# Cosformer attention and a multiplicative FFN on one core: the attention steps of batches 2 and 4 to 7 respaced within the FFN's steps

## The chip, the cores and the metric

The kernel runs on one core of one Trainium2 chip. The metric is the device time of one execution in microseconds; the time of a kernel is the median of several executions. Before the change it is 248.72 us, the median of 4 runs from 247.82 to 250.03 us.

## The reference

Inputs are q, k, v of shape (8 batches, 8 heads, 576 positions, 64) in float32 and four weight matrices. Attention is linear (no softmax), with cosine and sine weights by position; its output, 4608 tokens of 512, goes through three matrix products.

```python
def phi(x, c, s):
    r = np.maximum(x, 0.0)
    return np.concatenate([r * c, r * s], axis=-1)       # 64 -> 128 features
q_p = phi(q, cos_w, sin_w)
k_p = phi(k, cos_w, sin_w)
kv = np.einsum('bhsf,bhsd->bhfd', k_p, v)
z = np.sum(k_p, axis=2)
num = np.einsum('bhsf,bhfd->bhsd', q_p, kv)
den = np.einsum('bhsf,bhf->bhs', q_p, z)[..., None] + 1e-06
x = (num / den)                                          # tokens x 512
h = (x @ w1) * (x @ w2) @ w3
out = h @ w_out
```

## The kernel before

The 4608 tokens are 9 FFN tiles of 512. `ffn_groups` (L459) yields once for each step of a tile: 40 steps for tile 0 (which also multiplies w3 by w_out once, w34b), 24 for every other. In a tile from the third on, steps 0 to 15 are the two products of the eight 128-wide blocks in turn (w1b at an even step, w2b at an odd one, L465, four matmuls of 512 columns each) and steps 16 to 23 are the outputs of four blocks of 128 tokens in two halves each (L535, again four matmuls a step: the blocks jc 0 to 3, then 4 to 7 of abT). After a w1b step ScalarE copies the product from PSUM to asb (L518); after a w2b step VectorE multiplies the two into abT (L522); after every second output step ScalarE copies the block to osb (L542). FFN products take their PSUM banks from four in rotation.

Step numbers run through all tiles: tile 1 has the steps 40 to 63, tile 2 those from 64, tile 3 from 88, tile 4 from 112, and so on. The attention of a batch is spread over these steps by hand. `at(s, call)` (L562) puts a call into the list of step s; the loop at the end (L664) runs each step of the FFN and then the calls of that step, so the engines' queues get the instructions in this order. There is no other scheduler. Calls of one step stand in the order in which the plans were made: a batch's own in the order of `plan`, an earlier batch's ahead of a later one's.

`plan` (L572) places a batch's work in five chunks of 128 positions (the last has 64); odd batches begin with the short one:

- `kf`: `prep_k`, features of a k chunk. VectorE makes the cosine half (L273), ScalarE the sine half (L277).
- `qf`: `prep_q`, the same for a q chunk, and then `transpose_q`, a DMA transpose into qpT issued from SyncE's queue (L286).
- `vc`: `prep_v`, the copy of a v chunk into va, on GpSimd from batch 2 on (L300).
- `kv`: `kv_chunk`, eight matmuls on TensorE (L308) accumulated over the five chunks; after the last, ScalarE and VectorE copy the result to kvs (L313, L314).
- `nu`: `num`, the numerators of a chunk: eight matmuls on TensorE with qpT as weights and kvs moving (L368), and on VectorE the division by the denominators (L384 to L386) into xblk; then `x_tr`, a DMA transpose of xblk into the FFN's input xT, again from SyncE (L416).

`plan_loads` (L584) places the six loads of a batch, two halves each of k, q and v (for batch 3 the order is q, k, v). A load is issued from GpSimd's queue (L123, L127; batch 7: L133, L137), behind `hold_back` (L565): ScalarE writes one element, `mark` (L568), and GpSimd copies it, `seen` (L570), so that the load leaves no earlier than ScalarE comes to that place in its queue. Chunks 0 to 3 need both halves of a load, the short chunk one (batch 7: chunks 0 to 3 the first load, the short one the second). k and v have one buffer, q two.

For batches 4 to 7 the steps are given relative to two bases: `last`, the first numerator step of the batch before, and `base`, that of the batch itself (74, 99, 123, 148, 173).

Of the kernel before, what the change touches and what calls it, by code (L numbers as in the profile page):

```python
# [68 lines left out]
def kernel(  # L69
# [41 lines left out]
    def load(b, which, part=None):  # L111
        for name in which:
            src = {"k": k, "v": v, "q": q}[name]
            if b == B - 1:
                if part == 0:
                    raw[b, name] = ld.tile([P, H, NCH, D], BF16, name=name + "s",
                                           bufs=2 if name == "q" else 1)
                (load_first4 if part else load_first)(nc.gpsimd, raw[b, name], src, b=b)
                continue
            if part != 1:  # L120
                raw[b, name] = ld.tile([P, H, NCH, D], BF16, name=name + "s",
                                       bufs=2 if name == "q" else 1)
                nc.gpsimd.dma_start(  # L123
                    out=raw[b, name][0:64, :, :, :].rearrange("p h j d -> p h (j d)"),
                    in_=src[b, :, 0:320, :].rearrange("h (p j) d -> p h (j d)", j=5))
            if part != 0:
                nc.gpsimd.dma_start(  # L127
                    out=raw[b, name][64:128, :, 0:4, :].rearrange("p h j d -> p h (j d)"),
                    in_=src[b, :, 320:S, :].rearrange("h (p j) d -> p h (j d)", j=4))
# [116 lines left out]
    def order_of(b):  # L246

        return [0, 1, 2, 3, 4] if b % 2 == 0 else [4, 0, 1, 2, 3]
# [40 lines left out]
    def prep_k(b, c):  # L289
        features(b, feat_of(b)[0], raw[b, "k"], c)  # L290

    def prep_q(b, c):
        features(b, feat_of(b)[1], raw[b, "q"], c)
        if c in dma_q(b):
            transpose_q(b, c)

    def prep_v(b, c):
        R = ROWS[c]
        eng = nc.vector if b < 2 else nc.gpsimd
        eng.tensor_copy(out=feat_of(b)[2][:R, c, :, 0:D], in_=raw[b, "v"][:R, :, c, :])  # L300

    def kv_chunk(b, c, i):
        kp, qp, va = feat[b]
        if i == 0:
            att_of(b)["kv"] = ps_att.tile([P, 2, 512], FP32, name="pnum")
        kvt = att[b]["kv"]
        for h in range(H):
            nc.tensor.matmul(kvt[:, h // 4, ds((h % 4) * 65, 65)], lhsT=kp[:, c, h, :],  # L308
                             rhs=va[:, c, h, 0:D + 1], start=(i == 0 and h % 4 == 0),
                             stop=(i == NCH - 1 and h % 4 == 3))  # L310
        if i == NCH - 1:
            kvs = sm.tile([P, H, D + 1], BF16, name="kvs", bufs=2)
            nc.scalar.copy(out=kvs[:, 0:4, :], in_=kvt[:, 0, 0:260])  # L313
            nc.vector.tensor_copy(out=kvs[:, 4:8, :], in_=kvt[:, 1, 0:260])  # L314
            att[b]["kvs"] = kvs
# [88 lines left out]
    def x_tr(b, c, by_vector=False):  # L404
        R, rows = ROWS[c], out_rows(b, c)
        xblk = att[b]["x"].pop(c)
        xf = xblk[:].rearrange("p g h d -> p (g h d)")
        if b % 2 == 0:
            slot = S * b + 128 * c
        else:  # L410
            slot = S * b + (0 if c == 4 else 64 + 128 * c)
        t, o = divmod(slot, 512)
        if t not in xT:
            xT[t] = xtp.tile([P, 4, 512], BF16, name="xT")
        if b >= 2 or (b, c) in ((0, 4), (1, 3)):
            nc.sync.dma_start_transpose(out=xT[t][:, :, ds(o, R)], in_=xf[rows])  # L416
            return
        pst = ps_tr.tile([P, 8, 128], BF16, name="pst")
        for kc in range(4):
            nc.tensor.transpose(pst[:, kc, :], xf[:, ts(kc, 128)], identb[:])  # L420
        copy = nc.vector.tensor_copy if by_vector else nc.scalar.copy
        copy(out=xT[t][:, :, ds(o, R)], in_=pst[:, 0:4, rows])
# [139 lines left out]
    def at(s, *calls):  # L562
        slots[s] += calls

    def hold_back():  # L565

        mark = sm.tile([P, 1], BF16, name="mark", bufs=8)
        nc.scalar.copy(out=mark[0:1, :], in_=zeros[0:1, 0:1])  # L568
        seen = sm.tile([P, 1], BF16, name="seen", bufs=1)
        nc.gpsimd.tensor_copy(out=seen[0:1, :], in_=mark[0:1, :])  # L570

    def plan(b, kf, vc, kv, qf, nu, loads=None, xt=None):  # L572
        order = order_of(b)
        for i, c in enumerate(order):
            at(kf[i], lambda c=c: prep_k(b, c))
            at(qf[i], lambda c=c: prep_q(b, c))
            at(vc[i], lambda c=c: prep_v(b, c))
        for i, c in enumerate(order):
            at(kv[i], lambda c=c, i=i: kv_chunk(b, c, i))
        for i, c in enumerate(order):  # L580
            at(nu[i], lambda c=c: num(b, c, in_two=b == 1 and c in (0, 2)))
            at(xt[i] if xt else nu[i], lambda c=c: x_tr(b, c, by_vector=(b, c) == (1, 1)))

    def plan_loads(b, when):  # L584

        for piece, s in zip([(n, half) for n in {2: "kv", 3: "qkv"}.get(b, "kqv") for half in range(2)], when):
            def issue(piece=piece):
                hold_back()
                load(b, *piece)
            at(s, issue)  # L590
# [42 lines left out]
    for jp, s in enumerate((12, 16, 18, 20, 22, 24, 26, 28)):  # L633
# [3 lines left out]
         qf=(29, 30, 30, 31, 31), nu=(35, 36, 38, 39, 42), xt=(37, 38, 40, 42, 42))  # L637
    for c, s in zip(order_of(1), (31, 32, 34)):
        at(s, lambda c=c: q_tr(1, c))
    at(43, no_more_by_pe)  # L640
    plan_loads(2, (27, 28, 33, 35))
    plan(2, kf=(37, 39, 40, 41, 43), vc=(41, 42, 43, 44, 45), kv=(47, 47, 47, 48, 48),
         qf=(41, 42, 44, 45, 46), nu=(49, 51, 53, 55, 58))
    plan_loads(3, (36, 37, 47, 50, 54, 57))
    plan(3, kf=(54, 57, 59, 61, 63), vc=(64, 65, 66, 67, 68), kv=(71, 72, 72, 73, 73),
         qf=(60, 62, 64, 67, 70), nu=(74, 77, 79, 84, 87))

    bases = [74, 99, 123, 148, 173]
    for b, last, base in zip(range(4, B), bases, bases[1:]):
        plan_loads(b, [last + s for s in (-8, -5, 1, 4, 7, 10)])  # L650
        plan(b, kf=[last + s for s in (4, 7, 10, 13, 15)],
             vc=[base + s for s in (-9, -8, -7, -6, -5)],
             kv=[base + s for s in (-4, -3, -3, -2, -2)],
             qf=[base + s for s in (-12, -9, -6, -3, 0)],
             nu=[base + s for s in (0, 2, 5, 8, 11)])

    for i in range(2 * (NT - 1)):
        def put(i=i):
# [41 lines left out]
```

## Time and profile before

| what | value |
|---|---|
| runs | 247.82, 247.9, 249.55, 250.03 us; median 248.72 |
| profiled execution | 250.03 us, span 248.0 us from its first to its last instruction |
| TensorE granted clock | 0.999 of full |
| TensorE busy | 238.8 us, 96% of the span, 1842 matmuls |
| VectorE, ScalarE, GpSimd busy | 55%, 52%, 38% |
| DMA | 41.22 MB, mean 166 GB/s; loads (software queue) 73.7%, transposes (hardware queue) 34.1% of 16 engines' span |
| q and x transposes from SyncE | 33 and 32, median 4.4 and 4.9 us from issue to landing |
| loads of 320 KB (k, q, v) | median 6.3, 6.1 and 6.1 us from issue to landing |

Busy time of each engine, in stretches of 12.4 us (columns: the stretch, its length, busy us and number of instructions of TensorE, its weight loads, VectorE, ScalarE and GpSimd, the granted clock, the DMA engines' share and rate):

```profile
62.00:74.40 12.40, 12.35 (x144) 9.59 (x143) 10.10 (x25) 8.88 (x18) 4.27 (x9) 1.00 0.91 136
74.40:86.80 12.40, 11.48 (x73) 5.49 (x73) 8.22 (x23) 7.25 (x15) 3.04 (x7) 1.00 1.38 173
86.80:99.20 12.40, 12.29 (x97) 6.46 (x98) 6.31 (x12) 6.65 (x15) 4.58 (x10) 1.00 0.99 134
111.60:124.00 12.40, 12.29 (x105) 6.58 (x106) 8.06 (x17) 7.15 (x15) 5.34 (x11) 1.00 1.28 154
124.00:136.40 12.40, 11.76 (x75) 5.59 (x74) 7.28 (x20) 7.09 (x15) 3.36 (x8) 1.00 1.43 139
136.40:148.80 12.40, 12.29 (x105) 6.61 (x106) 7.54 (x18) 7.37 (x16) 4.78 (x11) 1.00 1.18 136
```

Between the first 12 us and the last, a stretch has 12.29 to 12.35 us of TensorE work, but for the two from 74.4 and from 124.0. Where an instruction stands in time is read from the timeline: tile 1 begins near 61 us, tile 2 (step 64) near 86, tile 3 (step 88) near 109.5, tile 4 (step 112) at 133.4, and batch 2's five numerators start at 71.5, 73.6, 75.6, 78.5 and 81.4 us.

### The profile page before, as it was taken

How to read it: one execution, taken by the hardware profiler on the slowest of the kernel's cores; microseconds unless marked ns; L12 is line 12 of the kernel's file. 1: busy time of each engine (PE TensorE's matmuls, PEld its weight loads, DVE VectorE, ACT ScalarE, POOL GpSimd, SP SyncE). 2: the span in 40 equal slices, each digit the busy share in tenths (PEclk: the TensorE clock that was granted, in tenths of full speed). 3: DMA queues.
4: the chain of work that ended last, by engine and by line, in shares of the span. 5: the costliest groups of instructions: out<-in, count | busy, mean ns of one | idle time of the engine just before them, and what ended most of it. 6: DMA issues, size and time to landing. Idle time of an engine off the chain costs nothing.

```text
span 248.0 us, 5010 instructions
## 1 busy us (share of the span) xinstructions
PE 238.8 (96%) x1842; PEld 130.8 (53%) x1872; DVE 137.5 (55%) x344; ACT 130.0 (52%) x266; POOL 93.5 (38%) x196
## 2 busy tenths in 40 slices
PE   8799999999998999999998999999999999999994
PEld 3479555566964445455544555455545554444443
DVE  7775663668967545646664476557464635312420
ACT  2575324856943873466556744855575333434332
POOL 7555352124422261217032612263213005978700
PEclk9999999999999999999999999999999999999999
DMA  7999999999989969999999999999994536898923
GB/s 195 178 197 199 207 205 201 196 181 172 140 131 169 177 103 165 113 143 133 175 123 155 123 149 183 169 123 143 163 143 86 98 63 211 254 283 295 272 104 129
DMA packets 86201, 41.22 MB, mean 166 GB/s; under 512 B 53793, under 2 KB 82721, under 8 KB 86177
## 3 DMA queue, kind: packets, MB, share of 16 engines
q0 software_dynamic: 37008, 27.20, 73.7%
q1 hardware_dynamic: 49168, 13.71, 34.1%
q8 instruction: 14, 0.23, 0.4%
q14 instruction: 11, 0.08, 0.1%
HBM read 38.80 MB, written 9.44 MB: 194 GB/s over the span
## 4 chain that ended last, share of the span: by engine, by line
PE 89%; DMA 6%; issue 2%; DVE 1%; POOL 1%; ACT 0%; POOLq 0%
PE ffnps L465 47%; PE ffnps L535 24%; PE ffnps L240 6%; PE pnum L368 4%; PE pnum L308 3%; DMA qs<-in_q_dram 3%; DMA qpT<-qp 3%; PE pst L226 1%; PE pst L339 1%; PE pst L420 1%; PE ffnps L551 1%; POOL vs L133 0%; DVE xblk L386 0%; PE pfirst L368 0%; ACT asb L518 0%
## 5 line engine op out<-in xcount | busy, mean ns | idle before, releaser
L465 PE MATMUL ffnps<-xT,w2b 128*128 128x512 bf16 (+2 forms) x338 | 75.0, 344 | 0.4
L465 PE MATMUL ffnps<-xT,w1b 128*128 128x512 bf16 (+2 forms) x333 | 74.3, 343 | 1.1 <-issue 0.6
L522 DVE TENSOR_TENSOR abT<-asb,ffnps 128x512 bf16<-128x512 bf16 x64 | 43.9, 686 | 54.2 <-PE ffnps L465 53.7
L518 ACT CAST asb<-ffnps 128x512 bf16<-128x512 f32 x64 | 37.4, 584 | 51.5 <-PE ffnps L465 48.0
L535 PE MATMUL ffnps<-w34b,abT 128*128 128x512 bf16 x271 | 63.7, 379 | 0.4
L465 PEld LDWEIGHTS <-w2b 128*128 128x128 bf16 x344 | 31.2, 98 | 27.8
L465 PEld LDWEIGHTS <-w1b 128*128 128x128 bf16 x344 | 30.5, 98 | 26.3 <-issue 1.1
L570 POOL COPY seen<-mark 1x1 bf16<-1x1 bf16 x50 | 8.9, 178 | 85.4 <-ACT mark L568 85.4
L542 ACT COPY osb<-ffnps 128x512 f32<-128x512 f32 x35 | 20.5, 585 | 38.2 <-PE ffnps L535 37.2
L535 PEld LDWEIGHTS <-abT 128*128 128x128 bf16 x280 | 25.9, 98 | 27.6
L277 ACT ACTIVATE qp<-qs,sinv 128x512 bf16<-128x512 bf16 (+2 forms) x40 | 28.1, 716 | 1.8 <-DMA qs<-in_q_dram 1.8
L300 POOL COPY va<-vs 128x512 bf16<-128x512 bf16 (+1 forms) x30 | 17.8, 627 | 23.6 <-DMA vs<-in_v_dram 23.6
L386 DVE TENSOR_TENSOR xblk<-pnum,den 128x512 bf16<-128x512 f32 (+1 forms) x37 | 25.6, 691 | 1.3
L277 ACT ACTIVATE kp<-ks,sinv 128x512 bf16<-128x512 bf16 (+1 forms) x35 | 24.9, 718 | 0.0
L450 POOL DMA_DIRECT2D out_dram<-osb x42 | 22.1, 531 | 3.0 <-issue 2.0
L368 PEld LDWEIGHTS <-qpT 128*128 128x128 bf16 x320 | 15.3, 98 | 9.8 <-DMA qpT<-qp 1.3
L384 DVE TENSOR_SCALAR den<-pnum 128x8 f32<-128x8 f32 (+1 forms) x37 | 6.0, 163 | 22.0 <-PE pnum L368 21.8
L368 PE MATMUL pnum<-kvs,qpT 128*128 128x65 bf16 x296 | 15.8, 194 | 0.9 <-DMA qpT<-qp 0.8
L273 DVE TENSOR_SCALAR qp<-qs,cosv 128x512 bf16<-128x512 bf16 (+1 forms) x40 | 15.6, 398 | 0.7 <-DMA qs<-in_q_dram 0.6
L240 PE MATMUL ffnps<-woutb,w3T 128*128 128x512 bf16 x61 | 15.1, 379 | 0.2
L308 PEld LDWEIGHTS <-kp 128*128 128x128 bf16 x280 | 11.4, 98 | 4.3
L273 DVE TENSOR_SCALAR kp<-ks,cosv 128x512 bf16<-128x512 bf16 (+1 forms) x35 | 13.0, 377 | 0.8 <-DMA ks<-in_k_dram 0.8
(88 smaller groups left out, 182.8 us busy)
## 6 DMA issues: line engine op xcount, KB each, us to landing
out_dram<-osb POOLq DMA_DIRECT2D x16, 256.0 KB, 4.4
out_dram<-osb POOLq DMA_DIRECT2D x24, 128.0 KB, 3.9
qs<-in_q_dram POOLq DMA_DIRECT2D x8, 256.0 KB, 8.2
ks<-in_k_dram POOLq DMA_DIRECT2D x6, 320.0 KB, 6.3
qs<-in_q_dram POOLq DMA_DIRECT2D x6, 320.0 KB, 6.1
vs<-in_v_dram POOLq DMA_DIRECT2D x6, 320.0 KB, 6.1
ks<-in_k_dram POOLq DMA_DIRECT2D x6, 256.0 KB, 6.8
vs<-in_v_dram POOLq DMA_DIRECT2D x6, 256.0 KB, 5.5
```

Of the source, the lines that this page charges most:

```text
L240: nc.tensor.matmul(acc[:, :], lhsT=w3T[:, lc % 4, :], rhs=woutb[:, lc, :], start=(lc == 0), stop=(lc == 7))
L273: nc.vector.tensor_scalar(out=dst[:R, c, :, 0:D], in0=src[:R, :, c, :], scalar1=0.0, scalar2=cosv[:R, at:at + 1], op0=ALU.max, op1=ALU.mult)
L277: nc.scalar.activation(out=dst[:R, c, 0:n, D:F], in_=src[:R, 0:n, c, :], func=ACTF.Relu, scale=sinv[:R, at:at + 1], bias=0.0)
L308: nc.tensor.matmul(kvt[:, h // 4, ds((h % 4) * 65, 65)], lhsT=kp[:, c, h, :], rhs=va[:, c, h, 0:D + 1], start=(i == 0 and h % 4 == 0), sto ...
L368: nc.tensor.matmul(banks[h // 4][:, ds((h % 4) * 65, 65)], lhsT=qpT[:, h, ds(at, 128)], rhs=kvs[:, h, :], start=True, stop=True)
L386: nc.vector.tensor_tensor(out=xblk[rows, g], in0=n4[:, :, :, 0:D], in1=den[rows, g].unsqueeze(3).to_broadcast([R, G, 4, D]), op=ALU.mult)
L450: eng.dma_start(out=rows[:, :, cols], in_=osb[64 * i:64 * i + rows.shape[0], :, cols])
L465: nc.tensor.matmul(out, lhsT=w[:, kc, ts(jc, 128)], rhs=x[:, kc, tok], start=(kc == 0), stop=(kc == 3))
L518: nc.scalar.copy(out=asb[:], in_=aT[:, :])
L522: nc.vector.tensor_mul(out=abT[:, jc, :], in0=asb[:], in1=bT[:, :])
L535: nc.tensor.matmul(ops[:, :], lhsT=abT[:, jc, ts(ms, 128)], rhs=w34b[:, jc, :], start=(jc == 0), stop=(jc == 7))
L542: nc.scalar.copy(out=osb[:, ms % 2, :], in_=ops[:, :])
```

## The change

Only step numbers change. No instruction is added or removed.

- Batch 2: k features of its last chunk go from step 43 to 44, q features (and transpose) of the third chunk from 44 to 43; kv goes from 47, 47, 47, 48, 48 to 46, 46, 46, 47, 47; the numerators from 49, 51, 53, 55, 58 to 48, 50, 52, 57, 60.
- Batch 3: its k loads go from 47 and 50 to 48 and 51; kv from 71, 72, 72, 73, 73 to 71, 71, 72, 72, 72. Numerators and features stay.
- Batches 4 to 7, relative to their bases: k loads a step earlier, q loads two steps and one step later, v loads the same and a step earlier; k features a step or two earlier and, at the end, two steps apart; v copies one step later and two of them in one step; kv in two steps instead of three; q features every two steps from -10 to -2 instead of every three from -12 to 0; the second numerator a step after the first instead of two.

```diff
-    plan(2, kf=(37, 39, 40, 41, 43), vc=(41, 42, 43, 44, 45), kv=(47, 47, 47, 48, 48),
-         qf=(41, 42, 44, 45, 46), nu=(49, 51, 53, 55, 58))
-    plan_loads(3, (36, 37, 47, 50, 54, 57))
-    plan(3, kf=(54, 57, 59, 61, 63), vc=(64, 65, 66, 67, 68), kv=(71, 72, 72, 73, 73),
+    plan(2, kf=(37, 39, 40, 41, 44), vc=(41, 42, 43, 44, 45), kv=(46, 46, 46, 47, 47),
+         qf=(41, 42, 43, 45, 46), nu=(48, 50, 52, 57, 60))
+    plan_loads(3, (36, 37, 48, 51, 54, 57))
+    plan(3, kf=(54, 57, 59, 61, 63), vc=(64, 65, 66, 67, 68), kv=(71, 71, 72, 72, 72),
          qf=(60, 62, 64, 67, 70), nu=(74, 77, 79, 84, 87))
 
     bases = [74, 99, 123, 148, 173]
     for b, last, base in zip(range(4, B), bases, bases[1:]):
-        plan_loads(b, [last + s for s in (-8, -5, 1, 4, 7, 10)])
-        plan(b, kf=[last + s for s in (4, 7, 10, 13, 15)],
-             vc=[base + s for s in (-9, -8, -7, -6, -5)],
-             kv=[base + s for s in (-4, -3, -3, -2, -2)],
-             qf=[base + s for s in (-12, -9, -6, -3, 0)],
-             nu=[base + s for s in (0, 2, 5, 8, 11)])
+        plan_loads(b, [last + s for s in (-9, -6, 3, 5, 7, 9)])
+        plan(b, kf=[last + s for s in (3, 6, 9, 11, 13)],
+             vc=[base + s for s in (-8, -7, -6, -6, -5)],
+             kv=[base + s for s in (-3, -3, -2, -2, -2)],
+             qf=[base + s for s in (-10, -8, -6, -4, -2)],
+             nu=[base + s for s in (0, 1, 5, 8, 11)])
```

## The prediction

> **What bounds the kernel now.** I read the engines' busy times, then who waited for whom on TensorE, then the chain of waits, then the DMA view and the timeline around the one long wait.
>
> The page's first row:
>
> ```profile
> PE 238.8 (96%) x1842; PEld 130.8 (53%) x1872; DVE 137.5 (55%) x344; ACT 130.0 (52%) x266; POOL 93.5 (38%) x196
> ```
>
> TensorE works 238.8 of 248.0 us; the idle rest is 9.2 us. The view of waits on TensorE says where it lies:
>
> ```profile
> PE unread L186 <- DVE zeros L162: 1.2, 1, 1.2
> PE kva L325 <- DVE va L300: 1.2, 1, 1.2
> PE pnum L368 <- DMA qpT<-qp: 0.8, 1, 0.8
> PE ffnps L465 <- issue: 0.6, 1, 0.6
> PE pst L420 <- DVE xblk L386: 0.3, 1, 0.3
> PE pst L352 <- DVE qp L280: 0.2, 1, 0.2
> ```
>
> Four of the six are in the first 16 us, which the change leaves alone, as it leaves the 3.1 us after the last matmul (244.87 of 248.0). The two others, 0.8 at 78.54 and 0.6 at 133.38, are all that a new spacing can win: 1.4 us, 0.6%. So the question is less what it wins than what it makes late.
>
> The chain of waits, around the first of them:
>
> ```profile
> 70.34 0.58 ACT asb L518
> 70.92 7.58 DMA qpT<-qp
> 78.54 0.43 PE pnum L368 x8
> ```
>
> The fourth numerator of batch 2 (chunk 3, step 55) waits for a transpose issued at 70.92 that takes 7.58 us. The DMA view of 70 to 84 us (40 slices of 0.35 us) shows why:
>
> ```profile
> GB/s 207 185 156 215 212 140 68 22 38 55 121 141 169 178 182 194 243 241 319 232 7 5 10 55 184 180 189 179 189 255 240 290 213 203 205 199 194 256 125 59
> ...
> ks<-in_k_dram POOLq DMA_DIRECT2D x1, 320.0 KB, 6.3
> vs<-in_v_dram POOLq DMA_DIRECT2D x1, 320.0 KB, 5.7
> ks<-in_k_dram POOLq DMA_DIRECT2D x1, 256.0 KB, 6.7
> ```
>
> Two holes: at 72.1 to 73.5, when batch 3's first k load (issued 70.06) starts to move, the rate falls to 22 to 68; and at 77.0 to 78.05 it is 5 to 10 whatever is queued. The transposes of batch 2's chunks 1, 2 and 3 took 3.2, 5.4 and 7.6 us from issue to landing (68.21, 69.56 and 70.92).
>
> The timeline of 60 to 90 us shows what the k load waits for, and who waits for it:
>
> ```profile
> 69.14 0.19 ACT L568 COPY mark<-zeros 1x1 bf16<-1x1 bf16 x1
> 70.06 0.69 POOL L123 DMA_DIRECT2D ks<-in_k_dram  x1 [0.42 <-DVE abT L471]
> 72.93 0.58 ACT L518 CAST asb<-ffnps 128x512 bf16<-128x512 f32 x1 [1.70 <-PE ffnps L465]
> 73.41 0.19 ACT L568 COPY mark<-zeros 1x1 bf16<-1x1 bf16 x1
> 74.18 0.68 POOL L127 DMA_DIRECT2D ks<-in_k_dram  x1 [0.28 <-issue]
> 77.49 0.33 DVE L273 TENSOR_SCALAR kp<-ks,cosv 64x512 bf16<-64x512 bf16 x1
> 77.84 0.69 DVE L522 TENSOR_TENSOR abT<-asb,ffnps 128x512 bf16<-128x512 bf16 x1
> 78.81 2.75 PE L535 MATMUL ffnps<-w34b,abT 128*128 128x512 bf16 x12
> ```
>
> A load leaves when ACT, in its own order, reaches its mark. VectorE makes batch 3's first k feature (step 54) ahead of the product abT of step 55, and the output matmuls (L535) need that product at the last quarter of step 57.
>
> **The change part by part.** A step is four matmuls of 512 columns, 0.86 us in the chain. No instruction is added or removed, and SP's transposes keep their order.
>
> *Batch 2, kv at 46/47, first three numerators a step earlier, last two two steps later.* PE's work is permuted: nothing in itself. The second kv group ends at 69.95 instead of 70.84 (one step less before it), numerator 0 follows a step later, as before, so its small wait for kvs (0.07 us) stays. Numerators 0, 1, 2 come at 70.84, 72.83 and 74.87 (71.7, 73.75 and 75.74 less a step). Chunks 0 and 1 had landed by 68.08 and 71.4. Chunk 2 landed at 74.95, 0.08 too late; but the load that made the first hole now starts later (below), and with chunk 1's 3.2 us it lands at 72.8: 0. At its old 5.4 us: 0.1. Numerator 3 at step 57 comes after groups 53 to 57: 75.13 + 5 x 0.865 = 79.46, where chunk 3 landed at 78.5: **the 0.81 us go**. What hides the transpose then is 1 us; if that is gone too, the old wait comes back in part. Numerator 4 has 3 us (79.08 against 82.1). qf of chunk 2 a step earlier, ahead of k chunk 4: on SP the transpose stands behind others that issue back to back from 68.21, so 0. The later outputs belong to tile 3, due at step 88: 0.
>
> *Batch 3's k loads at 48 and 51 instead of 47 and 50.* The first mark now stands behind the asb copy of step 48, not of step 47. Step 48 ends at 70.84 (70.33, and the 0.51 us of two kv chunks that now lie before it), the copy takes 0.58, the mark overlaps its end as at 73.41, and POOL issues 0.77 us after a mark (73.41 to 74.18): 72.1 instead of 70.06. One step on paper, two us in time. The second load's mark stands behind the asb of step 50 as before: 74.18, 0. The first load lands at 72.1 + 6.3 = 78.4 by its own row, at 78.8 by the 6.7 us of the second load, which crossed the hole at 77 as the first one will now; I take 78.6. Then k feature 0.33, product 0.69, some 0.1 between: abT of step 55 is there at 79.7. PE, which no longer waits for numerator 3, ends step 55 at 77.73, step 56 at 78.6, and needs it after three matmuls of step 57, at 79.25: **a new wait of 0.5**. From below: at the 5.0 us of the fastest k loads (90.10 to 95.09) it lands at 77.1 and costs 0. From above: at the 8.1 us of the slowest (a q load, 125.54 to 133.68) it lands at 80.2 and costs 2.1. Behind the waiting feature on VectorE stand that product and the normalization of numerator 3, on ACT the next features; ACT's asb copy of step 64 would end near 88, and its bank is needed again at step 68, near 89: 0.
>
> *Batches 4 to 7, second numerator a step after the first.* TensorE's sum is the same. The second chunk must have landed one step earlier. In batch 4 it landed at 121.07 (7.1 us after 113.94); the numerator now comes at 121.41 + 0.865 - 0.3 = 122.0. The features go from step 90 to 91, the issue by 0 to 0.7 us: landing at 121.1 to 121.8, cost 0. At 8.3 us, the slowest transpose in the trace (124.99 to 133.29), 0.9. Batches 5, 6 and 7 landed at 140.49, 165.97 and 188.81 and need theirs at 146, 170 and 194, a step later than that still early by over 3 us: 0.
>
> *Query features every two steps, last one before the first output.* Five 0.72 us sines on ACT over 9 steps instead of 13; ACT is 52% busy and SP needs 1.24 us per transpose against 1.73 us between: 0. The transposes of chunks 2, 3 and 4 gain 0 to 2 steps.
>
> *kv at -3 and -2, vc and loads moved.* The first k half goes past the va copies on POOL's queue, the fifth va copy of a batch goes behind the second k load. In batch 4: mark near 112.4, load to 113.7, four copies of 0.65 to 116.3, second load to 117.5, copy to 118.1; its kv chunk comes at 116.42 + 2 x 0.865 + 4 x 0.26 - 0.3 = 118.9: 0, bounds 0 and 0.4 per batch. k features come a step earlier behind loads that also leave a step earlier; the tightest, batch 6, had 146.98 against 148: 0. q loads land up to two steps later, and the tightest has two in hand (batch 5: 133.7 and at most a step more, against 136.5): 0.
>
> *The 0.59 us at 133.38.* The profile names no releaser, so no edit is aimed at it; by its row I keep it, bounds -0.6 and 0. The Trainium skill ("Runtime: NRT & Kernel Launch", Instruction fetch mechanics) says that instructions come in 16 KiB blocks whose fetch is mostly hidden. If that wait were a fetch, loads that leave at another time could hide it, and the sum would be 0.6 lower.
>
> The Trainium skill ("DMA: Bandwidth & Descriptors", Issuing engines are not separate DMA queues) speaks against the moved load: POOL's loads and SP's transposes run on the same 16 engines and interleave. By it the move is a swap, what chunks 2 and 3 gain the k load pays, and the sum would be 0. The trace agrees that they collide (the hole at 72.1).
>
> **Sum.** -0.81 + 0.5 = -0.3. The profiled execution took 250.03 us (span 248.0), so 249.7; it was the slowest of four, 1.3 above their median of 248.72. Against the median: **248.4**.
>
> **Rivals.**
> - *Clean gain.* The k load lands by 78.0 (5.9 us) and nothing waits: 248.72 - 0.81 = 247.9; with the 0.6 gone too, 247.3. For it: 5.0 us in two batches. Against: its own 6.3 and the hole at 77.
> - *Slower: the k load is the new wait.* Place: step 57, through the k feature ahead of abT. It decides from the point where the new wait passes 0.81: landing after 78.9, 6.8 us or more. At 8.1 us: -0.81 + 2.1 = +1.3, 250.0. For it: the hole falls into it. Against: of the six 320 KB k loads only two took over 6.7, one of them in the crowded first 40 us.
> - *Second numerators wait.* Batch 4 by 0.9 on top of the sum: +0.6, 249.3. Against: three other batches have 3 us.
>
> **How the numbers follow.** Forecast (within -0.6 and +0.1) 0.42, clean gain 0.30, slower 0.18, second numerators 0.10. The range takes in the clean gain with the 0.6 and the spread of the runs, and the slower rival: 246.9 to 250.1. About 1% (2.5 us) is what a measurement of this kernel can tell from no change. Faster by that needs more than the 1.4 us there are: 0.04; slower by that needs both slow rivals at their ends, or a wait in each of the five batches: 0.06; within 1%: 0.90.
>
> **What would show it.** In the profile after: no wait of pnum (L368) for qpT near 79; the first k load of batch 3 issued near 72.1; a wait of L535 for abT (L522) near 79.3, 0.5 us, with VectorE's kp behind it waiting for ks. If that wait is missing, the load was faster than 6 us. Wrong altogether: waits of L368 in batches 4 to 7, of L308 for va, or PE busy time other than 238.8.

## The result and the profile after

The changed kernel takes 249.74 us (median of 41 runs, 247.93 to 253.28), the kernel before 248.35 us (62 runs, 247.42 to 252.05). The ratio is 1.0052, 95% interval 1.0036 to 1.0068: about 1.3 us slower. It lies inside the stated range and within the 1%, but on the other side of the forecast. One profile below (v copies by VectorE) is of an execution at a granted clock of 0.993, where the others have 0.998 to 1.000.

The page's first row of the changed kernel (span 248.3 us; its execution took 250.02):

```profile
PE 238.6 (96%) x1842; PEld 130.6 (53%) x1872; DVE 140.5 (57%) x344; ACT 130.7 (53%) x266; POOL 94.1 (38%) x196
```

TensorE's work is the same, as it had to be. VectorE is busy 3 us longer with the same 344 instructions: some of them took longer, which comes back below. The waits of TensorE in the changed kernel (who waited for whom, us in total, times, longest):

```profile
PE pnum L368 <- DMA qpT<-qp: 1.7, 2, 1.2
PE kva L325 <- DVE va L300: 1.3, 1, 1.3
PE unread L186 <- DVE zeros L162: 1.2, 1, 1.2
PE pst L420 <- DVE xblk L386: 0.3, 1, 0.3
PE ffnps L535 <- DVE abT L522: 0.3, 1, 0.3
```

The 0.8 us of batch 2 and the 0.6 us without a releaser are gone. In their place stand the wait for abT that was forecast, and two waits of numerators that were not. The chain of waits of the changed kernel (130 to 180 us) places these two:

```profile
136.03 2.27 DVE qp L273
138.30 0.05 issue
138.34 0.42 ACT qp L277
138.77 5.67 DMA qpT<-qp
144.44 0.14 issue
144.58 0.42 PE pnum L368 x8
...
161.97 8.48 DMA qpT<-qp
170.46 0.05 issue
170.50 0.43 PE pnum L368 x8
```

At 144.58 the first numerator of batch 5 starts 1.17 us late, at 170.50 the second one of batch 6 0.50 us late. In stretches of 12.4 us (columns as in the table before the change) the first shows as 11.18 us of TensorE work where 12.29 is the rule, and the stretch from 124.0 has its 12.29 back:

```profile
124.00:136.40 12.40, 12.29 (x78) 6.04 (x79) 7.00 (x18) 8.29 (x18) 4.19 (x10) 1.00 1.25 160
136.40:148.80 12.40, 11.18 (x100) 5.93 (x100) 8.90 (x17) 5.89 (x13) 3.84 (x9) 1.00 1.09 145
```

**Batch 2, as forecast.** The timeline of the changed kernel around step 57:

```profile
70.89 0.19 ACT L568 COPY mark<-zeros 1x1 bf16<-1x1 bf16 x1
...
71.81 0.69 POOL L123 DMA_DIRECT2D ks<-in_k_dram  x1 [0.42 <-issue]
...
78.14 0.34 DVE L273 TENSOR_SCALAR kp<-ks,cosv 64x512 bf16<-64x512 bf16 x1 [1.69 <-DMA ks<-in_k_dram]
...
78.41 0.67 DVE L522 TENSOR_TENSOR abT<-asb,ffnps 128x512 bf16<-128x512 bf16 x1
...
79.14 0.39 PE L535 MATMUL ffnps<-w34b,abT 128*128 128x512 bf16 x1 [0.34 <-DVE abT L522]
```

The load leaves at 71.81 (forecast 72.1) and lands 6.3 us later; VectorE's k feature waits 1.69 us for it, the product abT stands behind it, and the last matmul of the output step waits 0.34 us (forecast 0.5).

**Batch 5: a q feature of 2.3 us.** VectorE and GpSimd in the changed kernel, 133 to 147 and 132 to 141 us:

```profile
135.95 2.34 DVE L273 TENSOR_SCALAR qp<-qs,cosv 128x512 bf16<-128x512 bf16 x1
```

```profile
135.75 0.68 POOL L123 DMA_DIRECT2D ks<-in_k_dram  x1 [0.36 <-issue]
136.42 2.33 POOL L300 COPY va<-vs 64x512 bf16<-64x512 bf16 x4
138.70 0.18 POOL L570 COPY seen<-mark 1x1 bf16<-1x1 bf16 x1
```

and the same feature in the kernel before:

```profile
135.98 0.61 DVE L273 TENSOR_SCALAR qp<-qs,cosv 128x512 bf16<-128x512 bf16 x1
```

The features mostly take 0.34 to 0.8 us. Here one is in progress when GpSimd starts four v copies in an unbroken run, and it ends within 0.5 us of the run's end. In the kernel before no more than three copies stand in a row there, and they come after the feature. The changed vc steps (two copies in one step) make the longer run. The transpose behind this feature leaves at 138.77 instead of 137.40, and takes 5.67 us where it took 3.08. The Trainium skill ("GPSIMD Engine Reference", Key points) says that GpSimd shares its SBUF interfaces with VectorE, with contention for some VectorE instructions; the trace agrees and gives a size, 2.34 us in place of 0.61. It does not come every time, as a profile of the first experiment below shows.

**Batch 6: a transpose of 8.5 us.** The second chunk's transpose in the changed kernel (the tile's view; start in us, then issue to landing):

```profile
L286 SPq DMA_TRANSPOSE qpT<-qp x1: 1231/1231/1231, 162.0 to 162.0; - x1
...
DMA to landing us min/median/max: 8.5/8.5/8.5
```

and in the kernel before:

```profile
L286 SPq DMA_TRANSPOSE qpT<-qp x1: 1242/1242/1242, 161.6 to 161.6; - x1
...
DMA to landing us min/median/max: 4.4/4.4/4.4
```

It leaves 0.4 us later and lands 4.5 us later. What differs around it is batch 7's first k load, whose issues are these, in the changed kernel and in the one before:

```profile
L133 POOL DMA_DIRECT2D ks<-in_k_dram x1: 887/887/887, 161.0 to 161.0; - x1
```

```profile
L133 POOL DMA_DIRECT2D ks<-in_k_dram x1: 891/891/891, 162.5 to 162.5; - x1
```

The load used to leave 1.0 us behind the transpose, now it leaves 1.0 us ahead of it.

### The profile page after: what moved, and what is told of

It reads as the page before. It is cut to its first block, busy times and chain, and to the rows that moved or that the text cites. A ratio compares the mean times of both kernels' runs of the same rounds, so it can differ in the third digit from the quotient of the medians.

```text
span 248.3 us, 5010 instructions
## 1 busy us (share of the span) xinstructions
PE 238.6 (96%) x1842; PEld 130.6 (53%) x1872; DVE 140.5 (57%) x344; ACT 130.7 (53%) x266; POOL 94.1 (38%) x196
## 4 chain that ended last, share of the span: by engine, by line
PE 82%; DMA 11%; DVE 2%; issue 2%; POOL 1%; ACT 1%; POOLq 0%; DVEq 0%
PE ffnps L465 42%; PE ffnps L535 24%; DMA qpT<-qp 6%; PE ffnps L240 6%; PE pnum L368 4%; DMA qs<-in_q_dram 3%; PE pnum L308 3%; DMA ks<-in_k_dram 3%; PE pst L226 1%; DVE qp L273 1%; PE pst L339 1%; PE pst L420 1%; PE ffnps L551 1%; DVE abT L522 1%; POOL vs L133 0%
## 5 line engine op out<-in xcount | busy, mean ns | idle before, releaser
L465 PE MATMUL ffnps<-xT,w2b 128*128 128x512 bf16 (+2 forms) x339 | 75.2, 344 | 0.4
L465 PE MATMUL ffnps<-xT,w1b 128*128 128x512 bf16 (+2 forms) x333 | 74.3, 343 | 0.4
L465 PEld LDWEIGHTS <-w1b 128*128 128x128 bf16 x344 | 31.1, 98 | 27.3
L465 PEld LDWEIGHTS <-w2b 128*128 128x128 bf16 x344 | 30.9, 98 | 27.0
L368 PEld LDWEIGHTS <-qpT 128*128 128x128 bf16 x320 | 15.2, 98 | 10.7 <-issue 1.6
L273 DVE TENSOR_SCALAR qp<-qs,cosv 128x512 bf16<-128x512 bf16 (+1 forms) x40 | 19.6, 498 | 0.6 <-DMA qs<-in_q_dram 0.6
L368 PE MATMUL pnum<-kvs,qpT 128*128 128x65 bf16 x296 | 15.7, 194 | 1.7 <-DMA qpT<-qp 1.7
L273 DVE TENSOR_SCALAR kp<-ks,cosv 128x512 bf16<-128x512 bf16 (+1 forms) x35 | 12.3, 366 | 1.8 <-DMA ks<-in_k_dram 1.7
L308 PEld LDWEIGHTS <-kp 128*128 128x128 bf16 x280 | 10.7, 98 | 2.9
```

The source lines that it names most:

```text
L273: nc.vector.tensor_scalar(out=dst[:R, c, :, 0:D], in0=src[:R, :, c, :], scalar1=0.0, scalar2=cosv[:R, at:at + 1], op0=ALU.max, op1=ALU.mult)
L368: nc.tensor.matmul(banks[h // 4][:, ds((h % 4) * 65, 65)], lhsT=qpT[:, h, ds(at, 128)], rhs=kvs[:, h, :], start=True, stop=True)
L465: nc.tensor.matmul(out, lhsT=w[:, kc, ts(jc, 128)], rhs=x[:, kc, tok], start=(kc == 0), stop=(kc == 3))
```

## The experiments

The theory, "order": loads and transposes that used to pass one another now meet, because the k loads go a step earlier and the second q transposes a step later, so that transposes land late; the second numerators, a step earlier, then wait. The rivals: "deadline" (the second numerator a step earlier is itself the cost), "port" (GpSimd's runs of copies stop VectorE's features), and that the loss is the late k load of batch 3. Ratios are to the kernel before, runs on the same chip, with 95% intervals.

**Each half alone.**

```diff
 e1: plan(2), plan_loads(3), plan(3) as changed; batches 4 to 7 as before
 e2: batches 4 to 7 as changed; plan(2), plan_loads(3), plan(3) as before
```

> The edits of batches 2 and 3 alone, batches 4 to 7 as in the kernel before. If the loss is made in batches 4 to 7 (my theory), the wait for qpT near 78.5 (0.81 us) goes, a wait of 0.3 us for abT comes near 79, none after it: 0.4 us faster than before, ratio 0.998. Rival, the loss is batch 3's late k load: ratio 1.004 or more, with a wait of over 1 us near 79.

> The edits of batches 4 to 7 alone. My theory: all of the loss is here, waits of numerators for qpT in batches 5 and 6 as in the changed kernel (1.2 and 0.5 us), the wait near 78.5 still there: 1.5 us slower than before, ratio 1.006. Rival, loss in batch 2 and 3: ratio 1.000.

Measured: batches 2 and 3 alone 0.9983 (0.9952 to 1.0013), with a wait for abT of 0.41 us at 79.32 and none other after 20 us; batches 4 to 7 alone 1.0044 (1.0007 to 1.0081), with a numerator of batch 6 waiting 0.48 us. The loss is made in batches 4 to 7. The second kernel has batch 2 as before, and yet no wait near 78: the 0.81 us is not in every execution. Nor is the wait of batch 5, which I expected here at 1.2 us: this profile, of the fastest of the six runs, does not have it. The second q feature of batch 5 stands there beside a run of four copies as in the changed kernel, 0.47 us ahead of it, and takes 0.64 us:

```profile
135.42 0.64 DVE L273 TENSOR_SCALAR qp<-qs,cosv 128x512 bf16<-128x512 bf16 x1
```

```profile
135.89 2.35 POOL L300 COPY va<-vs 64x512 bf16<-64x512 bf16 x4
```

So copies that start during a feature do not always hold it. What decides it in an execution stays open.

**Second numerators back, and forward alone.**

```diff
 e5, on the changed kernel
-             nu=[base + s for s in (0, 1, 5, 8, 11)])
+             nu=[base + s for s in (0, 2, 5, 8, 11)])
 e8, on the kernel before
-             nu=[base + s for s in (0, 2, 5, 8, 11)])
+             nu=[base + s for s in (0, 1, 5, 8, 11)])
```

> The changed kernel with the second numerators of batches 4 to 7 back two steps after the first. Deadline theory (the second numerator comes too early): the waits in batches 5 and 6 go, ratio to before 0.998. Transpose theory (the transposes leave or land late, and in odd batches the first numerator, whose weights span 128 columns, reads the second chunk too): the 1.2 us of batch 5 stay, the 0.5 us of batch 6 go, ratio 1.002 to 1.004.

> The kernel before with one edit: the second numerators of batches 4 to 7 one step after the first. If the early numerator by itself costs (deadline theory): ratio 1.003 or more and waits for qpT in batches 4 to 6. If it costs only together with late transposes: second transposes land in 3 to 7 us as before, no wait, ratio 1.000.

Measured: back 1.0014 (0.9985 to 1.0044), batch 6's wait down to 0.13 us though its transpose still takes 8.8 us, and none in batch 5, where I expected the 1.2 us to stay (its second feature takes 0.64 us in this profile); forward alone 1.0015 (0.9982 to 1.0049), no wait in the profile, batch 6's transpose 3.9 us. By itself the earlier numerator has no cost that shows; it turns a late transpose into a wait.

**Loads back; q steps back.**

```diff
 e4, on the changed kernel
-        plan_loads(b, [last + s for s in (-9, -6, 3, 5, 7, 9)])
+        plan_loads(b, [last + s for s in (-8, -5, 1, 4, 7, 10)])
 e3, on the changed kernel
-             qf=[base + s for s in (-10, -8, -6, -4, -2)],
+             qf=[base + s for s in (-12, -9, -6, -3, 0)],
```

> The changed kernel with all loads of batches 4 to 7 back at their steps. Order theory: what makes batch 6's second transpose take 8.5 to 8.8 us is that batch 7's first k load now leaves 1.0 us ahead of it instead of 1 us behind it; with the loads back it takes 4.3 to 5 us, the wait in batch 6 goes, ratio to before 1.000 (0.998 with the gain of batch 2). Deadline theory (a second numerator that comes a step earlier than the transpose can): the latency may fall, but a wait stays; ratio 1.003. Port theory: the v copies' runs change with the loads, q features over 1.4 us become rarer.

> The changed kernel with the q features and transposes of batches 4 to 7 back at every three steps from base -12 to 0. Order theory: the second transpose leaves 0.9 us earlier, at about the time of the k load, latency 4.5 to 6 us in batch 6, no wait there: ratio 0.999 to 1.001. Rival (the loads are slow wherever they stand, the transposes' place does not matter): latency over 8 us and the wait stays, ratio 1.005.

Measured: loads back 0.9994 (0.9968 to 1.0020), no wait after 20 us, batch 6's transpose 4.5 us. The tile's view of that kernel:

```profile
L286 SPq DMA_TRANSPOSE qpT<-qp x1: 1232/1232/1232, 160.3 to 160.3; - x1
...
DMA to landing us min/median/max: 4.5/4.5/4.5
```

```profile
L133 POOL DMA_DIRECT2D ks<-in_k_dram x1: 898/898/898, 161.0 to 161.0; - x1
```

The loss is gone with the loads alone. With the q steps back 1.0022 (0.9992 to 1.0051): transpose and load leave together, 7.9 us, but the transpose is early enough for its numerator. My 4.5 to 6 us was too low, the ratio unclear. The port theory is not ruled out by this: a q feature of 1.45 us stays in batch 6, but the one of batch 5 that made the longest wait takes 0.34 us with the loads back; the run of four copies, which stands behind the load on GpSimd's queue, starts there at 136.72, after it has ended.

**v copies back; v copies on VectorE.**

```diff
 e7, on the changed kernel
-             vc=[base + s for s in (-8, -7, -6, -6, -5)],
+             vc=[base + s for s in (-9, -8, -7, -6, -5)],
 e9, on the changed kernel
-        eng = nc.vector if b < 2 else nc.gpsimd
+        eng = nc.vector if b < 2 or b >= 4 else nc.gpsimd
```

> The changed kernel with the v copies of batches 4 to 7 back at one a step from base -9. Port theory: q features over 0.9 us go or become rare, the second transpose of batch 5 leaves by 137 and no wait comes there; batch 6's 0.5 us stays: ratio 1.003. Order theory alone: nothing changes, ratio 1.005.

> The changed kernel with the v copies of batches 4 to 7 on VectorE instead of GpSimd (0.28 us each there, 20 of them). Port theory (an unbroken run of four GpSimd copies, 2.33 us, stops VectorE's q feature, which took 2.34 us from the same moment, and so the transpose behind it): no q feature over 0.8 us, the wait of batch 5 goes; batch 6's, whose transpose left in time and took 8.5 us, may stay at 0.5: ratio 1.000 to 1.002. Load theory (the k loads lie on the transposes): both waits stay, ratio 1.005. If VectorE becomes late with the products abT instead: ratio over 1.005.

Measured: v copies back 0.9984 (0.9959 to 1.0010), more than either theory gave; no q feature over 0.9 us in batches 4 to 6, but the copies stand on GpSimd's queue ahead of the first k load, which so leaves 0.4 us behind the transpose (161.21 against 160.81), and that takes 6.9 us. This run undoes both causes at once. On VectorE, 1.0041 (1.0004 to 1.0077): no q feature is long, and the loss stays, as does batch 6's 8.6 us. But batch 5's first numerator waits 2.77 us in this profile, more than in any other. Its waits, and the transpose that it waited for:

```profile
PE pnum L368 <- DMA qpT<-qp: 3.4, 2, 2.8
```

```profile
L286 SPq DMA_TRANSPOSE qpT<-qp x1: 1236/1236/1236, 136.7 to 136.7; - x1
...
DMA to landing us min/median/max: 8.9/8.9/8.9
```

GpSimd, rid of the copies, issued loads earlier (batch 6's second k load at 137.5 instead of 138.8, 0.85 us behind this transpose). So the waits come without long features too; but the edit moves loads as well, and how much of the changed kernel's loss is the port's and how much the order's is not separated by these runs.

**Both kernels once more.**

> The changed kernel once more, for a second profile. Order theory: batch 6's second transpose again leaves behind batch 7's first k load, over 8 us to landing, and TensorE waits there for 0.3 to 0.8 us; near 79 abT is 0.3 to 0.4 us late. If the waits of the first profile were an accident of that execution, neither shows.

> The kernel before once more, for a second profile. If the 0.81 us wait at 78.54 is a feature of every execution it shows again at 0.6 to 1.0 us; if it was an accident (the kernel with only batches 4 to 7 changed has the same batch 2 and did not show it) there is none over 0.3 us, and the span is about 246.3.

Measured: the changed kernel (250.9 us, span 249.0) shows all its waits again: abT 0.95 at 79.84, batch 5's first numerator 1.20 at 145.31, batch 6's second 0.47 at 171.21. The cause in batch 5 repeats too:

```profile
136.66 2.35 DVE L273 TENSOR_SCALAR qp<-qs,cosv 128x512 bf16<-128x512 bf16 x1
```

```profile
137.13 2.34 POOL L300 COPY va<-vs 64x512 bf16<-64x512 bf16 x4
```

The kernel before (248.82 us, span 247.1) waits 0.53 us in batch 2, now at the third numerator (75.95), and 0.22 us at 178.96; the 0.59 us at 133 is not there. Both rival readings of that wait were half right: it comes and goes with the execution.

**Narrow first numerators.** In an odd batch the short chunk lies in columns 0 to 63 of qpT, and `num` takes 128 columns as weights: 64 of them are the second chunk's, whose results are not used.

```diff
 e6, on the changed kernel, in num
+            if b % 2 == 1 and b > 1 and c == 4:
+                nc.tensor.matmul(banks[h // 4][0:64, ds((h % 4) * 65, 65)],
+                                 lhsT=qpT[:, h, ds(at, 64)], rhs=kvs[:, h, :],
+                                 start=True, stop=True)
+                continue
 e12, on the changed kernel
-             qf=[base + s for s in (-10, -8, -6, -4, -2)],
+             qf=[base + s for s in ((-10, -3, -3, -2, -2) if b % 2
+                                    else (-10, -8, -6, -4, -2))],
 e13: both
```

> The changed kernel with the first numerators of batches 3, 5 and 7 as matmuls of 64 output rows, whose weights are the short chunk's 64 columns alone. If that numerator waited for the second chunk because its 128 columns reach into it, no wait shows at the first numerator of batch 5, at most a smaller one at the second, a step later: ratio to before 1.003 where the changed kernel has 1.005. If the columns do not matter: as the changed kernel.

> The changed kernel with the q features of the second to fifth chunk of batches 5 and 7 pushed to base -3, -3, -2, -2, so that the second chunk's transpose lands late on purpose. If the first numerator of an odd batch reads the second chunk too: TensorE waits at the first numerator of batches 5 and 7, 1 to 4 us each, until the second transpose has landed. If it reads only its own chunk: it does not wait, the second numerator does, a step later.

> The same, and the first numerators of odd batches with weights of the short chunk's 64 columns alone. If the 128 columns were what made it wait: no wait at the first numerator of batches 5 and 7; the wait stands at the second, a step later and about 1.1 us shorter. If not: as without the narrow weights.

Measured: narrow alone 1.0040 (1.0015 to 1.0064), where I expected 1.003; in its profile the second transpose of batch 5 landed at 141.9, in time, so it tells nothing of the question. The late pair does. With 128 columns TensorE waits at the first numerator of batch 5, 0.94 us, for a transpose that landed at 144.26, though the short chunk's own had landed at 137.53; batch 7 waits 0.78 us at its first (I expected 1 to 4 us each). With 64 columns the first numerator of batch 5 runs at 143.58 and the second waits; in batch 7 the first runs at 194.37, ahead of the second transpose's landing at 195.09, and neither waits. The timelines of the two (L369 is the narrow matmul; the lines below it are L368 and L465 moved down by five):

```profile
144.40 0.42 PE L368 MATMUL pnum<-kvs,qpT 128*128 128x65 bf16 x8 [0.94 <-DMA qpT<-qp]
```

```profile
143.58 0.44 PE L369 MATMUL pnum<-kvs,qpT 128*64 128x65 bf16 x8
143.96 1.04 PE L470 MATMUL ffnps<-xT,w1b 128*128 128x512 bf16 x4
146.44 0.43 PE L373 MATMUL pnum<-kvs,qpT 128*128 128x65 bf16 x8 [1.44 <-DMA qpT<-qp]
```

The dependence is shown. The second wait is not shorter here as I expected, because the transpose happened to land at 146.39, two us later than in the other kernel.

**Batch 2 mended, and a combination.**

```diff
 e10: plan(2), plan_loads(3), plan(3) as changed, batches 4 to 7 as before, and
-    plan(3, kf=(54, 57, 59, 61, 63),
+    plan(3, kf=(55, 57, 59, 61, 63),
 e11: the changed kernel with that edit, and with loads and vc of batches 4 to 7 as before
```

> The edits of batches 2 and 3 alone, and batch 3's first k feature at step 55, behind the product abT of that step, instead of 54. If that feature waiting for its late load is what holds abT, the 0.34 to 0.41 us wait of L535 near 79 goes and no other comes: span 246.0, 0.4 us less than with the edits of batches 2 and 3 alone, ratio to before 0.9965. Rival, another wait takes its place: ratio 0.998.

> The changed kernel with loads and v copies of batches 4 to 7 back at their steps and batch 3's first k feature at step 55. What stays of the change in batches 4 to 7 is q features every two steps, k features and kv closer, second numerators a step after the first. If these cost only together with the moved loads and v copies: no wait after 20 us, no q feature over 0.9 us in batches 4 to 6, ratio 0.997. If they cost by themselves: ratio 1.000 or more, with waits for qpT in batches 5 and 6.

Measured: the mended batch 2 takes 247.64 us against 248.36, ratio 0.9970 (0.9947 to 0.9993), with runs from 247.42 to 248.15 only. It is faster than the kernel before and than the changed one. VectorE in its profile, 76 to 81 us: the product no longer stands behind the waiting feature.

```profile
77.33 0.69 DVE L522 TENSOR_TENSOR abT<-asb,ffnps 128x512 bf16<-128x512 bf16 x1 [0.94 <-PE ffnps L465]
78.42 0.34 DVE L273 TENSOR_SCALAR kp<-ks,cosv 64x512 bf16<-64x512 bf16 x1 [0.40 <-DMA ks<-in_k_dram]
```

The combination has 1.0021 (0.9991 to 1.0051), runs from 247.18 to 253.26; its profile shows no wait after 20 us, and one q feature of 1.33 us in batch 4. I expected 0.997, and none over 0.9 us. What the rest of the change in batches 4 to 7 costs by itself, if anything, stays open.

**All profiles together.** Batch 6's second q transpose against batch 7's first k load, by how long after the transpose the load is issued (17 profiles: both kernels twice, the others once):

```
load issued after the transpose, us    transpose, issue to landing, us
+1.0, +1.1 (before, twice)             4.4, 4.6
+0.7 (e1, e4, e8, e10, e11)            4.3, 4.5, 3.9, 4.6, 4.8
+0.4 (e7)                              6.9
 0.0 (e3)                              7.9
-1.0 (changed twice, e2, e5, e6,       8.5, 8.5, 8.5, 8.8, 8.4,
      e9, e12, e13)                    8.6, 8.8, 8.5
```

For this pair the order decides: 0.7 us of lead or more and the transpose takes 3.9 to 4.8 us, whatever else the kernel changes. In the last row TensorE waits for it at batch 6's second numerator in every profile, 0.37 to 0.77 us (e5, with that numerator a step later: 0.13). In batch 5 the order is worth less: the second transpose takes 3.1 us with batch 6's first k load 1.3 us or more behind it (before twice, e1, e8, e10) and 4.4 to 4.9 us with the load 1.3 us ahead (e2, e5, e6, e7), which is in time for its numerator; in e9, with the second load 0.85 us behind it as well, it takes 8.9. With the changed kernel's q steps TensorE waits in batch 5 in three profiles only: in that kernel's two, where the feature was held, and in e9.

## Why the prediction was wrong

- **Batch 2: right in mechanism, and mis-sized.** The wait for chunk 3 went; the k load left at 71.81 (said: 72.1) and landed at 78.1 (78.6); abT came late by 0.34 us, in the second profile by 0.95, with the edits of batches 2 and 3 alone by 0.41 (said: 0.5). The prediction's sign holds too ("If that wait is missing, the load was faster than 6 us"): of the eleven profiles with the new steps and the feature at step 54, seven have the wait, with loads of 6.1 to 6.9 us, and four do not, with loads of 5.8 to 5.95 us. But "the 0.81 us go" took one execution for all: the four profiles with the old batch 2 show 0.81, 0.53, 0 and 0 us. The part is worth -0.17% (interval -0.48 to +0.13), which fits the -0.3 us of the sum.
- **"The 0.59 us at 133.38":** kept with bounds; no other profile has it. It was an accident of that execution, and neither a gain nor a loss of the change.
- **"Batches 5, 6 and 7 landed at 140.49, 165.97 and 188.81 and need theirs at 146, 170 and 194, a step later than that still early by over 3 us: 0."** This step failed, in three places. It took the landing of before and added a step, as if the transpose's time stayed; in batch 6 it went from 4.4 to 8.5 us, because the same change moves a load from behind the transpose to ahead of it. It took the feature's time as fixed; in batch 5 it went from 0.61 to 2.34 us in both profiles of the changed kernel (2.35 in the second), and the transpose left 1.4 us late. And 146 was the wrong deadline for batch 5: its first numerator reads the second chunk's columns too, and stood at 143.4. Landings after: 144.44, 170.46 and 189.73. Cost 1.17 + 0.50 us where the prediction has 0. In batch 5 of this profile neither the late start nor the load alone makes the wait, by an estimate from these numbers: from 138.77 the old 3.08 us would have landed at 141.85, and from 137.40 the 4.4 to 4.9 us that it took behind the load where the feature was not held (e2, e5, e6, e7) by 142.3, both ahead of 143.4. The prediction's own sign of being "wrong altogether", waits of L368 in batches 4 to 7, came.
- **"kv at -3 and -2, vc and loads moved":** each edit was asked whether its own data comes in time, and it does: no wait of TensorE for va or k features shows in batches 4 to 7. The text even has the four copies in a row, and prices them for their own data alone. What the moved loads and copies do to other engines' work in the same stretch was not asked. Undone one at a time, the loads (0.9994) and the v copies (0.9984) both bring the time back under the changed kernel's interval, the second numerator (1.0014) and the q steps (1.0022) leave it unclear. Either of the first two undoes both causes in its profile: batch 5's feature takes 0.34 or 0.57 us, and batch 6's transpose leaves ahead of the load. The share of each cause in the 1.3 us stays open.
- **Batch 4,** the one that the prediction called tight, did not wait in any profile. Two bounds of the prediction are misread, without effect on the sum: the trace has slower transposes than "8.3 us, the slowest transpose in the trace" (8.46 and 8.78 us, issued at 49.5 and 52.8), and slower loads than the 8.1 us "of the slowest" (up to 13.8 us, issued at 33.2). And 73.75 less a step is 72.89, not 72.83.
- **The rivals.** "Second numerators wait" came nearest: numerators waited, but in other batches, the longer wait at a first numerator, and with nearly twice its price (1.67 us against 0.9); its chance, 0.10, rested on the three us of lead above. The rule of the Trainium skill that loads and transposes interleave on the same engines ("DMA: Bandwidth & Descriptors", Issuing engines are not separate DMA queues) was weighed for batch 2 and not carried to batch 6, where a load had been moved as well; there the trace agrees with it, at 8.5 us instead of 4.4.

## What to carry to other kernels

A transfer's time in a profile belongs to the order of issues around it: where a change moves two queues towards each other, compare their issue times before reading off a margin, and in one place here less than two microseconds of order were worth four of latency. A deadline is set by what an instruction reads, padding included, not by what it needs. And one profile is one execution: a wait of 0.8 us on a kernel that scatters by 2 us should be seen twice before it is counted as a gain; so should a wait before it is counted as the loss.

## What the runs showed of the hardware

- A VectorE feature (bf16, one tensor from SBUF) that was in progress when GpSimd began four copies back to back was held until near their end in both profiles of the changed kernel: 2.34 and 2.35 us beside runs of 2.33 and 2.34, against 0.61 in the kernel before. It is no rule: in two other profiles (e2, e6) copies began 0.47 us into the same feature, as there, and it took 0.64 and 0.63 us. With the copies on VectorE none took over 0.9 us.
- A 512 KB load issued 1.0 us ahead of a q transpose nearly doubles its time (8.4 to 8.8 us against 3.9 to 4.8 with the load 0.7 us or more behind it). With a 320 KB load 1.3 us ahead, in batch 5, it was 4.4 to 4.9 us against 3.1, and 8.9 in one profile with a second load 0.85 us behind it.
- In all four profiles with the old steps of batch 2 the DMA rate falls to between 1 and 12 GB/s for 1 us, beginning at 77.0 to 77.7, with a q transpose and a k load under way. What causes it was not tried.
